# Attention, mixture of experts and soft experts on one core: w2 loaded first, p and phi issued by ScalarE, another order of the last output tiles

## Chip, cores and metric

The kernel runs on one core of one Trainium2 chip. The metric is the time of one execution on the device, in microseconds (us). The engines are TensorE (PE in the profile; its weight loads PEld), VectorE (DVE), ScalarE (ACT), GpSimd (POOL) and SyncE (SP, which only issues DMAs here). ScalarE and GpSimd issue some DMAs as well.

## The reference, cut to what matters

```
q, k, v: (4, 8, 576, 64)   p: (4, 8, 32, 64)   N = 4*576 = 2304, D = 512, F = 1024
sm_attn(a, b, c) = softmax(0.125 * a b^T) c
pk  = sm_attn(p, k, v)                       # 32 packed rows per head
x   = sm_attn(q, pk, pk), heads side by side # (2304, 512)
P   = domain_probs / (sum + 1e-9)            # (2304, 4)
x   = sum over 4 experts e of P[:, e] * (relu(x @ w1[e]) @ w2[e])
lg  = x @ phi                                # (2304, 32): 8 experts of 4 slots
d   = softmax of lg over the 2304 rows, c = softmax of lg over the 32 slots
slots = d^T @ x, expert by expert: relu(slots @ m1[e]) @ m2[e]   # m1 (8, 512, 1024), m2 (8, 1024, 512)
out = c @ slots                              # (2304, 512)
```

All of it is float32.

## The kernel before, in words

The kernel never forms the output x of the first mixture. Its product with phi is taken through `wphi` = w2[e] @ phi, 32 columns per expert, so that the hidden rows `ht` of the first mixture go straight to the logits. The work falls into a head, a main stage and a tail.

**Head** (lines 906 to 1014). The four batches go through one after the other; the head does attention for batch 0, in two groups of four heads (`attention`, g = 0 and 1), up to the point where the main loop can begin. The group's steps are: `kf` turns k on VectorE, `sa` the scores of p with k, `mx`, `ex`, `norm` the softmax, `et` its transposes, `pv` the product with v, `pk` its packing, `qf` and `sb` the scores of q, then a second softmax whose result is the operand `a2`. Beside them stands the work on `wphi` (`wphi_ops`, line 257): for each of eight half experts (1 MB of w2 each) 16 transposes on TensorE in four groups of four (`turn`, line 268), a copy by ScalarE per group (`put`, line 275), 32 small matmuls with phi (`project`, line 283), a copy, one transpose (line 299) and a copy. Four buffers hold w2; the load of a later half expert is issued by SP when the projection of the one four places earlier has been made. What of the wphi work is not placed in the head (`rest`) is dealt out in the first slots of the main loop, two ScalarE steps a slot.

The order of the head is made by `place_ops` (line 214): every step has an engine, a cost in us, the steps it depends on, the PSUM banks it takes and gives, and a rank (0 attention, 1 the first step of the main loop, 2 wphi). It places at each turn the step that can begin first, on ties the lower rank; a step that depends on another engine's begins 0.2 us after it. The result is one fixed order for each engine's queue; on the chip each engine runs its queue in that order and waits by semaphores. Loads are steps of SP with 2.5 us per MB, in the order of lines 928 to 941, behind a step `start`. After the head's steps SP issues p and k of batch 1 and part of its v (lines 1011 to 1014).

**Main stage** (line 1063). 128 slots. In slot s, `mm1(s)` makes 128 hidden features of one batch and expert with 12 matmuls (line 633); every fourth slot `make_g` (line 589) multiplies the packed values with the next 1 MB half of w1, for the next four slots. There is one w1 buffer: the next half is issued (line 183, by ScalarE) as the last step of `make_g`, and in program order `make_g(1)` stands right behind `mm1(0)`. `logits`, the softmaxes and the pooling of the previous batch are spread over the slots.

**Tail** (line 1113 on). From the start of batch 3, SP streams 80 chunks of 512 KB (w2, m1, m2) into whatever buffers come free (`load_chunk`). The last product (`slot_outputs`, line 1270) has two parts of 256 output columns; the chunks of the first part come first, four chunks of the second part last. For each part the kernel copies the accumulated rows (`so_sb`), sums them over four blocks with `rep` (`sr`), scales (`rr`) and then makes six output tiles, each of six matmuls (line 1316), three copies (`drain`) and one write of 384 KB by SP. `busy(n)` are n transposes whose result nobody reads.

Every DMA that SP or ScalarE issues takes one of eight semaphores in turn, and its issue waits until the transfer that had that semaphore before has landed.

Of the kernel before, what the change touches and what calls it, by code (L numbers as in the profile page):

```python
# [18 lines left out]
def tile_packed_attention_moe_softmoe(  # L19
# [28 lines left out]
    FC = 512  # L48
# [109 lines left out]
            )  # L158
        raw["v", b, g] = t

    def load_p(b):
        t = att_pool.tile([128, 4, D], F32, tag="p", name=f"p{b}")
        for a in range(2):
            for r in range(2):
                sp.dma_start(
                    t[64 * a + 32 * r : 64 * a + 32 * r + 32],
                    p[b].rearrange("(gh a) m d -> a m gh d", a=2)[a],
                )
        raw["p", b] = t
# [41 lines left out]
            self.deps, self.take, self.give, self.rank = list(deps), take, give, rank  # L211
            self.end = None

    def place_ops(ops, lag=0.2):


        free, banks_at, left = {}, [0.0] * 6, list(ops)
        while any(o.rank < 2 for o in left):
            ready = []
            for n, o in enumerate(left):  # L220
                spare = 2 if o.rank == 2 and o.take else 0
                if any(d.end is None for d in o.deps) or o.take + spare > len(banks_at):
                    continue
                t = max([d.end + lag * (d.eng != o.eng) for d in o.deps], default=0.0)
                if o.take:
                    t = max(t, sorted(banks_at)[o.take - 1])
                ready.append((max(t, free.get(o.eng, 0.0)), o.rank, n, o))
            first = min(ready, key=lambda c: c[:3])
            for t, rank, n, o in sorted(ready, key=lambda c: c[1:3]):
                if o.eng == first[3].eng and rank < first[1] and t < first[0] + 0.5 * first[3].cost:  # L230
                    first = (t, rank, n, o)
                    break
            t, _, n, o = first
            o.end = free[o.eng] = t + o.cost
            banks_at = sorted(banks_at)[o.take :] + [o.end] * o.give
            o.fn()
            left.pop(n)
        return left
# [8 lines left out]

    w2_t = {}

    def load_w2(n, t):  # L250
        e, hf = divmod(n, 2)
        sp.dma_start(
            t, w2[e, FC * hf : FC * hf + FC, :].rearrange("(x p) d -> p x d", p=128)
        )
        w2_t[n] = t

    def wphi_ops(n, loaded, next_load, done):
# [49 lines left out]
        def add(eng, cost, fn, deps, key, **kw):  # L307
            ops.append(Op(0, eng, cost, fn, deps, rank=2, key=n + key, **kw))
            return ops[-1]

        puts = []
        for x in range(4):
            tr = add("PE", 0.47, lambda x=x: turn(x), [loaded], 0.1 * x, take=1)
            puts.append(add("ACT", 0.58, lambda x=x: put(x), [tr], 0.1 * x, give=1))
        pr = add("PE", 1.3, project, puts, 0.5, take=1)
        if next_load:
# [589 lines left out]
    with tc.manual_schedule():  # L906
# [18 lines left out]
                i = 2 * g + hp  # L925
                load_qk(src, nm, b, g, hp, at and at[:, S * i : S * i + S])

        load("start", 0.9, lambda: None)
        load(("p", 0), 0.2, lambda: load_p(0))
        load(("k", 0), 0.6, lambda: load_two(k, "k", 0, 0))  # L930
        load(("k", 1), 0.6, lambda: load_two(k, "k", 0, 1))
        for g in range(2):
            load(("v", g), 0.8, lambda g=g: load_v(0, g, flat[1][:, 1536 * g : 1536 * g + 1536]))
        load(("q", 0), 0.6, lambda: load_two(q, "q", 0, 0, flat[0]))
        load("w2", 1.0, lambda: load_w2(0, w2s[0]))
        load(("q", 1), 0.6, lambda: load_two(q, "q", 0, 1, flat[0]))
        load("phi", 0.1, lambda: sp.dma_start(phi_sb, phi.rearrange("(c p) s -> p c s", p=128)))
        load("w1", 1.0, load_w1)
        load("w2_1", 1.0, lambda: load_w2(1, w2s[1]))
        for n in range(2, W2_BUFS):  # L940
            load(f"w2_{n}", 1.0, lambda n=n: load_w2(n, w2s[n]))

        make_identity(nc, ident)
        act.activation(out=den, in_=ident[:, 0:1], func=AF.Exp)
# [7 lines left out]
            rep[:, 0:96].rearrange("p (a s) -> p a s", a=3),  # L952
            st_i.unsqueeze(1).to_broadcast([128, 3, 32]),
        )
        busy(24)
        def head_tmp(tag, name):
            g = int(name[-1])
            if tag == "kt":
# [4 lines left out]
            n = (6 if name[0] == "n" else 4) + g  # L963
            return flat[2][:, S * n : S * n + S]

        ops.append(Op(0, "DVE", 0.45, lambda: flip_p(0), [loads["p", 0]]))
        att0 = [
            attention(0, g, head_tmp, lambda stage: None, (dve, pool)[g], loads) for g in range(2)
        ]
# [22 lines left out]
        def done():  # L992
            wphi_done[0] += 1

        landed = [loads["w2"]] + [loads[f"w2_{n}"] for n in range(1, W2_BUFS)]
        for n in range(NCH):
            after = None
            if n + W2_BUFS < NCH:
                m = n + W2_BUFS
                after = Op(  # L1000
                    0, "SP", 2.5, lambda m=m: load_w2(m, w2s[m % W2_BUFS]), [], rank=2
                )
                landed.append(after)
            ops += wphi_ops(n, landed[n], after, done)
        rest = sorted(place_ops(ops), key=lambda o: o.key)
        for o in list(rest):
# [263 lines left out]
        def slot_outputs():  # L1270
# [21 lines left out]
                busy(3)  # L1292
            return ended

        for p, (d0, dw) in enumerate(parts):
            ended = p > 0
            while not ended:
                ended = slot_outputs()
            so_sb = leftover(1, dw, d0)
            act.copy(so_sb, so[:, d0 : d0 + dw])  # L1300
            sr = mm_ps(f"sr{d0}")
            pe.matmul(sr[:, :dw], rep, so_sb, start=True, stop=True)
            rr = end[:, CHUNK : CHUNK + dw]
            act.mul(rr, sr[:, :dw], -1.0)
            for b2 in range(NB // 2):
                rows = out[2 * b2 * S : 2 * (b2 + 1) * S, d0 : d0 + dw].rearrange(
                    "(r x) d -> r x d", x=XR
                )
                cv = ct[:, b2].rearrange("p x b r t -> p x (b r t)")
                for j0 in range(0, XR, nt):  # L1310
                    jn = min(XR - j0, nt)
                    ob = out_tile()
                    ps = [mm_ps(f"o{d0}_{b2}_{j0}_{j}", keep=True) for j in range(jn)]
                    for j in range(jn):
                        o = slice(32 * j, 32 * j + 32)
                        pe.matmul(  # L1316
                            ps[j][:, :dw], cv[o, j0 + j], rr[o], start=True, stop=True,
                            tile_position=(32 * j, 0),
                        )
                    for j in range(jn):  # L1320
                        drain(ob[:, dw * j : dw * j + dw], ps[j][:, :dw])
                    let_go(ps)
                    sp.dma_start(
                        rows[:, j0 : j0 + jn, :],
                        ob[:, : dw * jn].rearrange("p (j d) -> p j d", d=dw),
                    )
                    if p == 0:
                        busy(2)
            while p == 0 and ck < len(chunks):
                slot_outputs()  # L1330


# [28 lines left out]
```

## Time and profile before

| | us |
|---|---|
| median of 3 runs (lowest to highest) | 505.82 (504.54 to 507.71) |
| the profiled execution | 501.07 |
| its span, first to last instruction | 499.3 |

| engine | busy us | share of the span |
|---|---|---|
| TensorE | 475.2 | 95% |
| VectorE | 295.3 | 59% |
| GpSimd | 197.3 | 40% |
| ScalarE | 182.5 | 37% |

The shares are averages over the whole span. A matmul's end is modelled, so a busy TensorE need not be at its peak. The granted clock is given as a share of 2.4 GHz; 0.50 is 1.2 GHz.

### The profile page before, as it was taken

To read this page: it belongs to the slowest core of one execution; us is meant where nothing else is said; L and a number is where in the kernel's file an instruction comes from. 1 tells how busy PE (TensorE), PEld (TensorE's weight loads), DVE (VectorE), ACT (ScalarE), POOL (GpSimd) and SP (SyncE) were. 2 spreads that over 40 slices of the span, in tenths; PEclk is the share of its full clock that TensorE was granted. 3 is DMA by queue.
4 is the path that set the end of the run, shared out by engine and by line. 5 is a ranking of instruction groups with operands and counts; after the bars stand their busy time and mean duration, and the time that the engine had idled before them with its cause. 6 is when DMAs were issued, how large, how long until landed. Compare 5 with 4: busy or idle time off the path is not lost.

```text
span 499.3 us, 13307 instructions
## 1 busy us (share of the span) xinstructions
PE 475.2 (95%) x5625; PEld 330.7 (66%) x5625; DVE 295.3 (59%) x557; ACT 182.5 (37%) x451; POOL 197.3 (40%) x250
## 2 busy tenths in 40 slices
PE   7798999999999999999999999999999999898884
PEld 4667887777775767788567787776787965231142
DVE  4683456687881778797558798872767632320022
ACT  1466655444440444445224444431434210110033
POOL 3022433356842445675325467641567502100000
PEclk9789999999999999999999999999999999899998
DMA  8979932655231356652214622393762689999996
GB/s 196 380 256 350 299 133 87 199 148 158 85 126 46 134 177 146 181 170 85 87 63 160 177 85 86 106 346 142 269 237 89 251 325 413 413 418 415 397 304 222
DMA packets 54667, 104.35 MB, mean 209 GB/s; under 512 B 5904, under 2 KB 20752, under 8 KB 54608
## 3 DMA queue, kind: packets, MB, share of 16 engines
q1 hardware_dynamic: 41280, 77.15, 44.2%
q10 hardware_dynamic: 13200, 26.22, 15.5%
q8 instruction: 44, 0.72, 0.6%
q0 software_dynamic: 128, 0.15, 0.2%
q14 instruction: 15, 0.12, 0.1%
HBM read 98.78 MB, written 4.72 MB: 207 GB/s over the span
## 4 chain that ended last, share of the span: by engine, by line
PE 69%; DMA 16%; DVE 8%; ACT 2%; SPq 1%; POOL 1%; issue 1%; ACTq 0%
PE h L633 35%; PE pb L794 8%; DMA hr<-in_moe_w_dram 8%; PE g L598 6%; PE lg L666 6%; DMA ck<-in_moe_w_dram 6%; PE pv L468 2%; PE sb L371 2%; PE w2t L268 2%; PE o L1316 2%; DMA p<-in_p_dram 2%; DVE hr L654 2%; DVE g L610 1%; PE sa L371 1%; DMA hr<-in_v_dram 1%; PE pw L283 1%
## 5 line engine op out<-in xcount | busy, mean ns | idle before, releaser
L633 PE MATMUL h<-a,g 128*128 128x288 f32 x1536 | 224.5, 300 | 0.6 <-DVE a L555 0.6
L633 PEld LDWEIGHTS h<-a,g 128*128 128x128 f32 x1536 | 206.7, 188 | 26.8 <-issue 14.7
L644 POOL TENSOR_TENSOR ht<-ht,work 128x288 f32<-128x288 f32 x191 | 154.5, 818 | 175.2 <-ACT ht L643 174.9
L643 ACT ACTIVATE ht<-h 128x288 f32<-128x288 f32 x191 | 78.5, 412 | 164.7 <-PE h L633 148.8
L654 DVE STREAM_TRANSPOSE hr<-ht 128x576 f32<-128x576 f32 x128 | 97.6, 764 | 37.4 <-POOL ht L644 34.8
L610 DVE TENSOR_TENSOR g<-g,g 128x512 fp32r<-128x512 f32 x64 | 41.2, 684 | 34.5 <-ACT g L608 34.5
L608 ACT CAST g<-g 128x512 fp32r<-128x512 f32 x64 | 34.5, 589 | 24.4 <-PE g L598 24.4
L638 DVE SCALAR_TENSOR_TENSOR ht<-h,work 128x288 f32<-128x288 f32 x65 | 28.6, 440 | 24.5 <-PE h L633 24.2
L666 PE MATMUL lg<-ht,wphi 128*32 128x288 f32 x512 | 38.7, 412 | 0.0
L666 PEld LDWEIGHTS lg<-ht,wphi 128*32 128x32 f32 x512 | 14.0, 109 | 33.1 <-POOL ht L644 23.3
L598 PE MATMUL g<-w,pkn 64*32 64x512 f32 x512 | 35.0, 603 | 0.2 <-DMA w<-in_moe_w_dram 0.2
L794 PE MATMUL pb<-hr,work 32*32 32x512 f32 x864 | 30.6, 598 | 0.0
L1265 DVE COPY ob<-o 128x256 f32<-128x256 f32 x9 | 3.5, 420 | 33.9 <-PE o L1316 33.9
L275 ACT COPY hr<-w2t 128x512 f32<-128x512 f32 x32 | 17.9, 597 | 7.4 <-PE w2t L268 7.4
L268 PE MATMUL w2t<-ident,hr 128*128 128x128 f32 x128 | 19.2, 292 | 1.1 <-DMA hr<-in_moe_w_dram 0.9
L794 PEld LDWEIGHTS pb<-hr,work 32*32 32x32 f32 x864 | 12.6, 103 | 11.4 <-issue 8.7
L268 PEld LDWEIGHTS w2t<-ident,hr 128*128 128x128 f32 x128 | 15.2, 148 | 4.9 <-issue 1.2
L686 POOL COPY work<-dpn 128x576 f32<-128x576 f32 x16 | 10.9, 680 | 13.6 <-DVE dpn L202 13.6
L808 DVE SCALAR_TENSOR_TENSOR tacc<-tacc,rsc,pb 128x512 f32<-128x512 f32 x12 | 8.2, 744 | 13.6 <-PE pb L794 13.6
L1280 PE MATMUL so<-hr 128*32 128x512 f32 (+1 forms) x68 | 13.7, 553 | 2.5 <-DMA hr<-in_moe_w_dram 2.3
L122 PE MATMUL busy<-ident 128*128 128x128 f32 x85 | 13.7, 307 | 1.4 <-POOL ident masks.py:199 1.4
L122 PEld LDWEIGHTS busy<-ident 128*128 128x128 f32 x85 | 10.7, 157 | 6.1 <-issue 4.2
(176 smaller groups left out, 442.7 us busy)
## 6 DMA issues: line engine op xcount, KB each, us to landing
w<-in_moe_w_dram ACTq DMA_DIRECT2D x25, 1024.0 KB, 5.1
ck<-in_moe_w_dram SPq DMA_DIRECT2D x42, 512.0 KB, 8.6
hr<-in_moe_w_dram SPq DMA_DIRECT2D x32, 512.0 KB, 9.9
hr<-in_moe_w_dram SPq DMA_DIRECT2D x8, 1024.0 KB, 10.9
w<-in_moe_w_dram SPq DMA_DIRECT2D x7, 1024.0 KB, 5.1
k<-in_k_dram SPq DMA_DIRECT2D x16, 288.0 KB, 4.4
v<-in_v_dram SPq DMA_DIRECT2D x18, 192.0 KB, 5.4
q<-in_q_dram SPq DMA_DIRECT2D x12, 288.0 KB, 3.0
```

What stands on the lines that cost most here:

```text
L122: pe.transpose(wp[:, :128], ident, ident)
L268: pe.transpose(st[x][:, 128 * dc : 128 * dc + 128], t[:, x, 128 * dc : 128 * dc + 128], ident,)
L598: pe.matmul(ps[g][c : c + 32, :], pkn_t[b][o : o + 64, g, hp, 0, :], t[o : o + 64, 2 * g + hp, :], start=True, stop=True, tile_position=(o ...
L608: act.copy(gg[:, 0, g], ps[g])
L610: dve.tensor_tensor(out=gg[:, 1, g], in0=ps[g], in1=gg[:, 0, g].bitcast(F32), op=ALU.subtract)
L633: pe.matmul(ps[:, :HS], gg[:, l, g, fs], m[:, ts], start=(g == 0 and i == 0), stop=(g == 1 and i == 2),)
L638: dve.scalar_tensor_tensor(out=ht[:, ts], in0=ps[:, :HS], scalar=0.0, in1=pr[:, ts], op0=ALU.max, op1=ALU.mult,)
L643: act.activation(out=ht[:, ts], in_=ps[:, :HS], func=AF.Relu)
L644: pool.tensor_tensor(out=ht[:, ts], in0=ht[:, ts], in1=pr[:, ts], op=ALU.mult)
L654: dve.transpose(out=hr[:, place(b, i), :, f0 : f0 + 32], in_=ht_t[s].rearrange("p (x t) -> p x t", t=32),)
L666: pe.matmul(lg_t[b][r][32 * x : 32 * x + 32, :HS], wphi[:, NFT * e + 4 * hf + x, :], ht_t[4 * ci + x][:, HS * r : HS * r + HS], start=(ch ...
L794: pe.matmul(pb[c][m : m + 32, :], d[o, x + par, :], hr[o, lo : hi + 1 : hi - lo, x + par, :], start=(x == 0), stop=(x == NBLK - 2), tile_p ...
```

## The change

Head: p and phi are issued by ScalarE at the beginning (`load_p(0, act)` and one more issue) instead of by SP; SP begins with the first MB of w2 in two halves, then k of both groups, the second MB of w2, and then v and q group by group, the third MB of w2, w1, the fourth MB. The costs of the loads in the plan are changed, and a step that depends on a load is placed 1.8 us after it instead of 0.2. The first two groups of transposes of w2's first MB depend on its first half alone. The filler at the start has 14 transposes instead of 24.

Tail: the six fillers of two transposes between the first part's tiles go. The second part's products, and the copy of their sum, come ahead of the first part's last two tiles instead of behind them.

```diff
-    def load_p(b):
+    def load_p(b, eng=sp):
...
-    def place_ops(ops, lag=0.2):
+    def place_ops(ops, lag=0.2, land=1.8):
...
-                t = max([d.end + lag * (d.eng != o.eng) for d in o.deps], default=0.0)
+                t = max(
+                    [d.end + (land if d.eng == "SP" else lag * (d.eng != o.eng)) for d in o.deps],
+                    default=0.0,
+                )
...
-            tr = add("PE", 0.47, lambda x=x: turn(x), [loaded], 0.1 * x, take=1)
+            tr = add("PE", 0.47, lambda x=x: turn(x), [loaded[x // 2]], 0.1 * x, take=1)
...
-        load("start", 0.9, lambda: None)
-        load(("p", 0), 0.2, lambda: load_p(0))
-        load(("k", 0), 0.6, lambda: load_two(k, "k", 0, 0))
+        load("start", 1.0, lambda: None)
+        load("p", 0.0, lambda: None)
+        load("w2_0a", 0.55, lambda: load_w2(0, w2s[0], (0, 2)))
+        load("w2_0b", 0.55, lambda: load_w2(0, w2s[0], (2, 4)))
+        load(("k", 0), 0.8, lambda: load_two(k, "k", 0, 0))
         load(("k", 1), 0.6, lambda: load_two(k, "k", 0, 1))
-        for g in range(2):
-            load(("v", g), 0.8, lambda g=g: load_v(0, g, flat[1][:, 1536 * g : 1536 * g + 1536]))
+        load("w2_1", 1.05, lambda: load_w2(1, w2s[1]))
+        load(("v", 0), 1.0, lambda: load_v(0, 0, flat[1][:, :1536]))
         load(("q", 0), 0.6, lambda: load_two(q, "q", 0, 0, flat[0]))
-        load("w2", 1.0, lambda: load_w2(0, w2s[0]))
+        load(("v", 1), 1.0, lambda: load_v(0, 1, flat[1][:, 1536:3072]))
         load(("q", 1), 0.6, lambda: load_two(q, "q", 0, 1, flat[0]))
-        load("phi", 0.1, lambda: sp.dma_start(phi_sb, phi.rearrange("(c p) s -> p c s", p=128)))
-        load("w1", 1.0, load_w1)
-        load("w2_1", 1.0, lambda: load_w2(1, w2s[1]))
-        for n in range(2, W2_BUFS):
-            load(f"w2_{n}", 1.0, lambda n=n: load_w2(n, w2s[n]))
+        load("w2_2", 1.05, lambda: load_w2(2, w2s[2]))
+        load("w1", 1.05, load_w1)
+        load("w2_3", 1.05, lambda: load_w2(3, w2s[3]))
+        load_p(0, act)
+        act.dma_start(phi_sb, phi.rearrange("(c p) s -> p c s", p=128))
...
-        busy(24)
+        busy(14)
...
+        def take_slots(d0, dw):
+            so_sb.append(leftover(1, dw, d0))
+            act.copy(so_sb[-1], so[:, d0 : d0 + dw])
+
+        while not slot_outputs():
+            pass
+        take_slots(*parts[0])
         for p, (d0, dw) in enumerate(parts):
-            ended = p > 0
-            while not ended:
-                ended = slot_outputs()
-            so_sb = leftover(1, dw, d0)
-            act.copy(so_sb, so[:, d0 : d0 + dw])
             sr = mm_ps(f"sr{d0}")
-            pe.matmul(sr[:, :dw], rep, so_sb, start=True, stop=True)
+            pe.matmul(sr[:, :dw], rep, so_sb[p], start=True, stop=True)
...
-                    if p == 0:
-                        busy(2)
-            while p == 0 and ck < len(chunks):
-                slot_outputs()
+                if p == 0 and n == len(tiles) - 3:
+                    while ck < len(chunks):
+                        slot_outputs()
+                    take_slots(*parts[1])
```

## Rows read from the trace of the kernel before

**Rows 1.** Stretches of 20 us: length, each engine's busy time, granted clock, DMA share, GB/s
```profile
60.00:80.00 20.00, 20.00 (x242) 16.77 (x241) 9.69 (x17) 10.82 (x26) 7.80 (x10) 1.00 0.29 105
...
380.00:400.00 20.00, 20.00 (x180) 17.06 (x181) 12.90 (x23) 6.85 (x16) 12.73 (x16) 1.00 0.51 190
```

**Rows 2.** Chain of waits, 36 to 45 and 385 to 424: start, us, what
```profile
36.71 7.78 DMA p<-in_p_dram
...
44.57 0.40 ACTq L183
...
413.27 10.45 DMA hr<-in_moe_w_dram
```

**Rows 3.** Timeline, TensorE and ScalarE's issues, 19 to 47: start, us, what, [idle before]
```profile
19.40 2.82 PE L268 MATMUL w2t<-ident,hr 128*128 128x128 f32 x12 [0.92 <-DMA hr<-in_moe_w_dram]
...
28.23 1.23 PE L598 MATMUL g<-w,pkn 64*32 64x512 f32 x16
...
29.39 1.53 PE L268 MATMUL w2t<-ident,hr 128*128 128x128 f32 x12
...
30.85 1.08 PE L283 MATMUL pw<-hr,tacc 128*32 128x128 f32 x32
...
33.93 0.43 ACTq L183 DMA_DIRECT2D w<-in_moe_w_dram  x1
...
39.26 1.86 PE L633 MATMUL h<-a,g 128*128 128x288 f32 x12
...
41.35 1.09 PE L598 MATMUL g<-w,pkn 64*32 64x512 f32 x16 [0.23 <-DMA w<-in_moe_w_dram]
...
46.13 1.06 PE L283 MATMUL pw<-hr,tacc 128*32 128x128 f32 x26 [1.05 <-ACT hr L275]
```

**Rows 4.** Shorter stretches, columns as in rows 1
```profile
2.00:6.00 4.00, 3.82 (x23) 3.58 (x21) 0.45 (x1) 0.23 (x2) 3.39 (x9) 1.00 0.77 166
26.00:28.00 2.00, 2.00 (x56) 0.74 (x36) 1.00 (x3) 0.00 (x0) 0.00 (x0) 0.50 1.05 402
428.00:430.00 2.00, 1.08 (x8) 0.97 (x8) 0.75 (x1) 0.00 (x0) 0.00 (x0) 1.00 1.03 416
431.40:434.70 3.30, 3.30 (x20) 0.85 (x16) 1.18 (x4) 1.74 (x4) 1.16 (x1) 0.50 1.02 406
```

**Rows 5.** DMA issues at 17.7, at 33.9, whole span: count, KB, us to landing
```profile
hr<-in_moe_w_dram SPq DMA_DIRECT2D x1, 1024.0 KB, 13.8
...
w<-in_moe_w_dram ACTq DMA_DIRECT2D x1, 1024.0 KB, 7.3
...
w<-in_moe_w_dram ACTq DMA_DIRECT2D x25, 1024.0 KB, 5.1
```

**Rows 6.** Costliest groups, whole span: count | busy us, mean ns | idle before
```profile
L275 ACT COPY hr<-w2t 128x512 f32<-128x512 f32 x32 | 17.9, 597 | 7.4 <-PE w2t L268 7.4
```

**Rows 7.** Timeline of TensorE, 478 to 494, columns as in rows 3
```profile
478.29 0.71 PE L1316 MATMUL o<-work,hr 32*128 32x256 f32 x6 [0.47 <-ACT work L1304]
...
485.02 1.93 PE L1280 MATMUL so<-ck,hr 128*32 128x256 f32 x32
487.45 0.70 PE L1302 MATMUL sr<-hr,rep 128*128 128x256 f32 x2 [0.49 <-ACT hr L1300]
488.62 4.55 PE L1316 MATMUL o<-work,hr 32*128 32x256 f32 x36 [0.47 <-ACT work L1304]
```

**Rows 8.** DMA issues at 473.2, 485.4, 490.0 and 493.7, columns as in rows 5
```profile
ck<-in_moe_w_dram SPq DMA_DIRECT2D x2, 512.0 KB, 8.6
...
out_dram<-hr SPq DMA_DIRECT2D x1, 384.0 KB, 4.1
...
out_dram<-hr SPq DMA_DIRECT2D x1, 384.0 KB, 2.4
...
out_dram<-work SPq DMA_DIRECT2D x1, 384.0 KB, 4.1
```

More of the change, by code (lines that the diff above doesn't have):

```diff
@@ L164, in load_p @@
             for r in range(2):
-                sp.dma_start(
+                eng.dma_start(
                     t[64 * a + 32 * r : 64 * a + 32 * r + 32],
@@ L248, in tile_packed_attention_moe_softmoe, with load_w2 @@
     w2_t = {}
-    def load_w2(n, t):
+    def load_w2(n, t, xs=(0, 4)):
         e, hf = divmod(n, 2)
+        xs = slice(*xs)
         sp.dma_start(
-            t, w2[e, FC * hf : FC * hf + FC, :].rearrange("(x p) d -> p x d", p=128)
+            t[:, xs],
+            w2[e, FC * hf : FC * hf + FC, :].rearrange("(x p) d -> p x d", p=128)[:, xs],
         )
@@ L964, in head_tmp @@
             return flat[2][:, S * n : S * n + S]
-        ops.append(Op(0, "DVE", 0.45, lambda: flip_p(0), [loads["p", 0]]))
+        ops.append(Op(0, "DVE", 0.45, lambda: flip_p(0), [loads["p"]]))
         att0 = [
@@ L993, in done @@
             wphi_done[0] += 1
-        landed = [loads["w2"]] + [loads[f"w2_{n}"] for n in range(1, W2_BUFS)]
+        landed = [(loads["w2_0a"], loads["w2_0b"])]
+        landed += [(loads[f"w2_{n}"],) * 2 for n in range(1, W2_BUFS)]
         for n in range(NCH):
@@ L1002, in tile_packed_attention_moe_softmoe @@
                 )
-                landed.append(after)
+                landed.append((after, after))
             ops += wphi_ops(n, landed[n], after, done)
@@ L1293, in slot_outputs @@
             return ended
-        for p, (d0, dw) in enumerate(parts):
-            ended = p > 0
-            while not ended:
-                ended = slot_outputs()
-            so_sb = leftover(1, dw, d0)
-            act.copy(so_sb, so[:, d0 : d0 + dw])
+        so_sb = []
+        def take_slots(d0, dw):
[4 more added lines that the diff above has]
+        take_slots(*parts[0])
+        for p, (d0, dw) in enumerate(parts):
             sr = mm_ps(f"sr{d0}")
-            pe.matmul(sr[:, :dw], rep, so_sb, start=True, stop=True)
+            pe.matmul(sr[:, :dw], rep, so_sb[p], start=True, stop=True)
             rr = end[:, CHUNK : CHUNK + dw]
             act.mul(rr, sr[:, :dw], -1.0)
-            for b2 in range(NB // 2):
+            tiles = [(b2, j0) for b2 in range(NB // 2) for j0 in range(0, XR, nt)]
+            for n, (b2, j0) in enumerate(tiles):
                 rows = out[2 * b2 * S : 2 * (b2 + 1) * S, d0 : d0 + dw].rearrange(
@@ L1309, in tile_packed_attention_moe_softmoe @@
                 cv = ct[:, b2].rearrange("p x b r t -> p x (b r t)")
[L1310 to L1325, printed above, removed]
-                    )
-                    if p == 0:
-                        busy(2)
-            while p == 0 and ck < len(chunks):
-                slot_outputs()
+                jn = min(XR - j0, nt)
+                ob = out_tile()
+                ps = [mm_ps(f"o{d0}_{b2}_{j0}_{j}", keep=True) for j in range(jn)]
+                for j in range(jn):
+                    o = slice(32 * j, 32 * j + 32)
+                    pe.matmul(
+                        ps[j][:, :dw], cv[o, j0 + j], rr[o], start=True, stop=True,
+                        tile_position=(32 * j, 0),
+                    )
+                for j in range(jn):
+                    drain(ob[:, dw * j : dw * j + dw], ps[j][:, :dw])
+                let_go(ps)
+                sp.dma_start(
+                    rows[:, j0 : j0 + jn, :],
+                    ob[:, : dw * jn].rearrange("p (j d) -> p j d", d=dw),
+                )
+                if p == 0 and n == len(tiles) - 3:
+                    while ck < len(chunks):
+                        slot_outputs()
+                    take_slots(*parts[1])
 _INS = ['q', 'k', 'v', 'p', 'moe_domain_probs', 'moe_w1', 'moe_w2', 'moe2_phi', 'moe2_w1', 'moe2_w2']
```

## Prediction

> **What bounds the kernel now.** I read the table of stretches first. From 60 us on TensorE is busy for 20.00 of 20 us [rows 1], and so it stays to about 400 us, so any real work that TensorE no longer has to do there, and any earlier start of that stage, comes off the end. Next the chain of waits. After 413.27 us it runs through DMAs alone [rows 2]: the stream of 512 KB chunks that feeds the last three products. That stream is started by buffers which the end of the main stage frees, so it moves as a whole with the main stage. Thus two stretches are left in which time can be won by ordering: the head, up to where the main loop runs without gaps (about 47 us), and the tail, from the landing of the first part's last chunk (476 us) to the last write.
>
> In the head the timeline shows TensorE waiting for data and then doing it in an unlucky order: at 19.40 it had waited 0.92 us for the first MB of w2, spends 2.82 us on twelve transposes of it, and only then begins group 1's product with v, which was ready [rows 3]. The DMA engines are the other half: 402 GB/s at a share of 1.05 when full, but a share of only 0.77 from 2 to 6 us [rows 4], about 4 x (1 - 0.77/1.05) = 1.07 us of transfer time unused. In the tail, the second part's 32 products stand behind all six output tiles of the first part and then pay a copy, a sum over slots and a scaling with nothing beside them [rows 7], while the writes stop between the two parts [rows 8].
>
> **Head, the order.** I followed place_ops with the new costs. On TensorE it gives: all 16 transposes of w2's first half MB pair and their projection, first part of attention (with one wait for phi ahead of it), 16 transposes of w2's second MB among the attention steps, the second projection, g of step 0, then 16 + 12 more transposes and two more projections, and mm1(0). Before, 15 groups of four transposes and three projections stood ahead of mm1(0); now 19 and four.
>
> **Head, work moved ahead.** Four more groups are 16 transposes at 1.53/12 = 0.13 us [rows 3]: 2.0 us. One more projection is 1.08 us [rows 3]. Together 3.1 us, which the main loop, where TensorE is never idle, no longer has. This counts in full if the time at which the main loop reaches a given point does not move.
>
> **Head, start of the loop.** The block of 0.92 + 2.82 us disappears from between the two products with v, a gain of at most 3.7 us for mm1(0), before at 39.26 [rows 3]. Against it, 1 MB of w2 now stands ahead of k and another ahead of v and q: at 402 GB/s each is 2.6 us; phi's 64 KB come on top, 1.07 us are won back. mm1(0) thus lies between 35.5 and about 39.5; I take 37.5. It is not what decides.
>
> What decides is make_g(1), right behind mm1(0) on TensorE, which needs the second half MB pair of w1. That load can be issued only after g of step 0 has used the one w1 buffer. The first w1 load is now followed by one MB only (w2's fourth). Before, the last load of the head landed at 17.7 + 13.8 = 31.5 us [rows 5]; with 1.07 us less idling it lands at 30.5, so w1 at 27.9, and g of step 0 stays at about 28.2, where it was [rows 3]. The next w1 issue was 5.7 us behind g, at 33.93 [rows 3]; ScalarE now has one w2 copy more ahead of it, 0.6 us [rows 6]: 34.5. It took 7.3 us to land, beside w2 loads on SP's queue [rows 5], and again has w2 loads beside it (the fifth, sixth and seventh, which no longer wait for a projection). So g(1) starts at 41.8, before at 41.35 [rows 3]: **a loss of 0.45 us**. Bounds of this landing: 5.1 us, the median over all ScalarE w1 loads [rows 5], which would put it at 39.6; and one further MB ahead of it, 2.6 us, which puts it at 44.4.
>
> **Head, one wait goes.** At 46.13 a projection had waited 1.05 us for a copy by ScalarE [rows 3], because ScalarE stood still until it could issue the third w1 load at 44.57, released by a p load that took from 36.71 to 44.5 [rows 2]. Those p loads now follow the seventh w2 load on SP, which is released by the third projection some 34 us in, and land before ScalarE comes to that issue. **1.05 us gained**; bound below 0 if p is as late again.
>
> **Head, the clock.** mm1(0) takes 1.86 us [rows 3] and ends at 39.4, so TensorE idles 2.4 us until g(1). In the window from 428 TensorE was busy for 1.08 of 2 us, and from 431.4 to 434.7 the granted clock was 0.50, which is 1.2 GHz [rows 4]. I expect the same fall here. Twelve transposes took 2.82 us at 0.50 and 1.53 at 1.00 [rows 3], so a stretch of 3.3 us at the lower level does the work of 1.8 us: **a loss of 1.5 us**; bounds 0 and 3 (two such stretches). The Trainium skill (TensorE: Matmul & The Clock Gate, HAM oscillation) ties the fall to waits for DMA longer than this one; by it the clock would hold and the sum be 1.5 us better. The 0.92 us without a matmul in the window from 428 were shorter and the clock still fell, so I keep the term.
>
> Head: 3.1 - 0.45 + 1.05 - 1.5 = 2.2 us.
>
> **Head, edits at nothing.** p and phi by ScalarE: five issues of 0.43 us [rows 3] and the table load behind them, ahead of ScalarE's first copy, which waits for w2 until about 5 us; that wait hides them, and without it they would cost about 2 us of ScalarE. SP loses those five issues. The warm-up of 14 instead of 24 transposes ends where w2's first half lands; if that lands late, the first transposes run at the lower level while TensorE waits for k anyway.
>
> **Tail.** Before, the first tile of part one begins at 478.29 and that of part two at 488.62: 10.33 us [rows 7]. After: four tiles at the pace of part two, which has no filler, 4.55/6 = 0.76 us: 3.0 us. Then 32 products, 1.93 us; their last chunk lands at 473.2 + 8.6 = 481.8 [rows 8], just as they get to it. Two more tiles, 1.5 us, which now cover the copy of the second part. Then the slot sum 0.70 and the scaling, 0.47 until the next tile as in [rows 7]: 1.2 us. Sum 7.6, so part two starts 2.7 us earlier on TensorE. The writes give some of that back. The last six land from 490.0 + 2.4 to 493.7 + 4.1 [rows 8], one per 1.07 us, slower than TensorE makes them; and the sixth write of part one landed at 485.4 + 4.1 = 489.5. If the first six end there again, the seventh lands at 490.6 instead of 492.4: 1.9 us. If they go out as fast as they are made, 2.7. I take 2.2 us, nearer to the row. With the six fillers gone the products and tiles themselves keep TensorE running.
>
> **Sum.** 2.2 + 2.2 = 4.4 us. The profiled execution took 501.07 us (span 499.3 and 1.8 around it), 0.9% under the median of the runs shown, 505.82; I take the 4.4 us off the median: **501.4 us**.
>
> **Rivals.** (a) The clock holds while TensorE waits for g(1): 5.9 us gained, 499.9. For it: ahead of 46.13 TensorE idled 1.05 us and the next 26 matmuls took 1.06 us, near the 1.08 us of 32 at 30.85 and not twice that [rows 3]; against it the fall after 428 [rows 4]. (b) w1's second load lands like the others, 5.1 us: g(1) follows mm1(0) at 39.6, a gain of 1.75 in place of a loss of 0.45 and no fall: 8.1 us, 497.7. Against it: SP's queue is full at that time. (c) The head gives nothing: a half-speed stretch falls on group 1's attention from about 22 us, as it did from 18 to 28 (0.50 at 26 us, [rows 4]), g(0) and everything behind it slip by 2 us; or writes give back the whole tail. About 2.2 us left: 503.6. (d) Slower: the early w2 loads delay w1. If the queues are served in the order of issue instead of taking turns, the second w1 load sits behind two MB of w2, 2 x 2.6 us, and lands at 47. g(1) loses 5.65 instead of 0.45, TensorE sits through two half-speed stretches, 3 us: head 3.1 + 1.05 - 5.65 - 3.0 = -4.5, with the tail 2.3 us slower: 508.1. It is slower than before from a landing at about 45 us. Against it: the p load on SP and the w1 load on ScalarE were in flight together, and w1, issued at 33.93 behind a w2 MB, landed in 7.3 us.
>
> **Chances.** The forecast 0.50, (a) 0.24, (b) 0.10, (c) 0.10, (d) 0.06. A measurement of this kernel can tell about 1% from no change, 5.06 us. (a) and (b) pass that, the forecast only at its upper edge: faster by over 1% 0.36, within 1% 0.58, slower by over 1% 0.06 at most, the end of (d). The range takes in (b) and (c) and the bounds of g(1): 497.7 to 505.0.
>
> **What would show it.** The transposes of w2's first MB lie before the first scores of attention; mm1(0) near 37.5; a gap in front of g(1) that a w1 load ends, near 41.8; the granted clock at 0.50 within 4 us behind it, or not; no gap before the fourth or fifth projection; part two's first tile 7.6 us behind part one's; the last write 1.9 to 2.7 us closer to the landing of the first part's last chunk. The prediction is wrong if TensorE does not wait for w1 at g(1), if phi's load holds up the first projection and with it the scores, or if the main stage shows new gaps.

## The result and the profile after

The changed kernel takes 504.29 us (median of 20 runs, 501.48 to 506.95), the kernel before 501.75 us beside it (20 runs, 497.62 to 507.71). The ratio is 1.0058, with the 95% interval [1.003, 1.0085]: slower by 0.6%, where 0.9% faster was forecast. Ratios leave out executions that took over 1.5% more than the fastest of their kernel. The profiled execution took 505.59 us with a span of 503.8, against 501.07 and 499.3.

The chain of waits of the changed kernel, 15 to 60 us, has two DMAs that the same stretch of before had not (start, us, what):

```profile
13.31 9.50 DMA hr<-in_v_dram
22.95 2.78 PE pv L473 x48
...
30.78 0.84 DVE hr L518 x2
...
34.80 0.79 DVE hr L549
...
36.25 2.04 ACT hr L280 x4
38.29 0.35 ACT g L613
38.68 9.88 DMA w<-in_moe_w_dram
48.69 1.96 PE g L603 x16
```

Between the two the chain runs through the second softmax of group 1 on VectorE, which begins late because the product with v was late, and through the copies and the cast that ScalarE has to make before it comes to the issue. The timeline of TensorE and ScalarE's issues shows the two DMAs as idle time of TensorE (start, us, what, [idle before]); the rows answer to [rows 3]:

```profile
4.52 2.62 PE L273 MATMUL w2t<-ident,hr 128*128 128x128 f32 x16
8.95 1.08 PE L288 MATMUL pw<-hr,tacc 128*32 128x128 f32 x32 [1.82 <-DMA tacc<-in_moe_phi_dram]
...
22.95 2.78 PE L473 MATMUL pv<-hr 96*64 96x32 f32 x48 [4.18 <-DMA hr<-in_v_dram]
...
27.76 1.78 PE L288 MATMUL pw<-hr,tacc 128*32 128x128 f32 x32
...
31.30 1.09 PE L603 MATMUL g<-w,pkn 64*32 64x512 f32 x16
...
36.88 0.66 PE L273 MATMUL w2t<-ident,hr 128*128 128x128 f32 x4 [1.73 <-ACT hr L280]
...
38.68 0.45 ACTq L183 DMA_DIRECT2D w<-in_moe_w_dram  x1
...
41.09 1.86 PE L638 MATMUL h<-a,g 128*128 128x288 f32 x12
48.69 1.96 PE L603 MATMUL g<-w,pkn 64*32 64x512 f32 x16 [5.74 <-DMA w<-in_moe_w_dram]
...
51.56 2.55 PE L638 MATMUL h<-a,g 128*128 128x288 f32 x12
```

What to see: the transposes of w2's first MB do lie early, but 4.18 us of waiting for v have taken the place of the block of 0.92 + 2.82 us that stood before group 1's product with v [rows 3]. g of step 0 is at 31.30 instead of 28.23, the second w1 load is issued at 38.68 instead of 33.93, and g(1) begins at 48.69 instead of 41.35 after a wait of 5.74 us. Short stretches show the clock and the DMA engines there (length, busy of PE, PEld, DVE, ACT, POOL, granted clock, DMA share, GB/s), as [rows 4]:

```profile
22.42:29.25 6.83, 6.30 (x108) 4.72 (x112) 3.87 (x10) 0.62 (x3) 0.67 (x1) 0.50 1.05 400
36.00:38.00 2.00, 1.12 (x24) 0.95 (x28) 1.93 (x6) 2.00 (x5) 1.13 (x1) 1.00 0.01 3
38.00:40.00 2.00, 2.00 (x34) 1.66 (x25) 1.85 (x3) 1.76 (x5) 0.35 (x1) 1.00 0.24 22
...
42.00:44.00 2.00, 0.95 (x8) 0.71 (x6) 0.00 (x0) 1.63 (x5) 0.59 (x1) 1.00 1.01 377
...
46.32:53.14 6.82, 4.45 (x27) 2.81 (x28) 1.80 (x3) 1.82 (x4) 0.00 (x0) 0.50 0.97 242
60.00:80.00 20.00, 20.00 (x238) 16.30 (x237) 9.92 (x16) 11.37 (x26) 7.21 (x9) 1.00 0.27 98
...
483.22:490.05 6.83, 6.83 (x52) 3.91 (x53) 2.45 (x6) 2.14 (x6) 0.00 (x0) 0.50 0.86 281
```

The clock falls to 0.50, the level of 1.2 GHz, within each of the two gaps (at 22.42 and at 46.32), and once in the tail. From 60 us on TensorE is as full as before [rows 1]. The DMA issues at 13.3 and 38.7 us and over the whole span, as [rows 5] (KB, us to landing):

```profile
hr<-in_v_dram SPq DMA_DIRECT2D x1, 192.0 KB, 9.5
...
w<-in_moe_w_dram ACTq DMA_DIRECT2D x1, 1024.0 KB, 9.9
...
w<-in_moe_w_dram ACTq DMA_DIRECT2D x25, 1024.0 KB, 5.1
```

The tail on TensorE, as [rows 7]:

```profile
483.01 4.50 PE L1328 MATMUL o<-work,hr 32*128 32x256 f32 x24 [0.47 <-ACT work L1316]
487.45 3.19 PE L1288 MATMUL so<-ck,hr 128*32 128x256 f32 x32
490.57 1.85 PE L1328 MATMUL o<-work,hr 32*128 32x256 f32 x12
492.35 0.70 PE L1314 MATMUL sr<-hr,rep 128*128 128x256 f32 x2
493.58 4.54 PE L1328 MATMUL o<-work,hr 32*128 32x256 f32 x36 [0.53 <-ACT work L1316]
```

The order is the new one, but 24 matmuls take 4.50 us where 36 take 4.54, and the 32 products 3.19 us instead of 1.93: they ran at the lower level. From the first part's first tile to the second part's it is 10.57 us, before 10.33.

To add it up I use a mark in the main loop, the start of mm1's group 16 (of its 128 of 12 matmuls each): 91.88 us before, 96.94 after. From group 8 to group 16 it is 26.78 us before and 23.91 after, so the work moved ahead is worth 2.9 us. Group 8 itself begins at 65.10 and at 73.03, 7.9 us later. And from the landing of the first part's last chunk to the end of the span ("tail" below) it is 23.35 us before and 23.13 after.

### The profile page after: what moved, and what is told of

Read it like the earlier page. It is cut to its first block, busy times and chain, and to the rows that moved or that the text cites. A ratio compares the mean times of both kernels' runs of the same rounds, so it can differ in the third digit from the quotient of the medians.

```text
span 503.8 us, 13274 instructions
## 1 busy us (share of the span) xinstructions
PE 474.0 (94%) x5603; PEld 330.7 (66%) x5603; DVE 295.2 (59%) x557; ACT 182.8 (36%) x451; POOL 197.1 (39%) x250
## 4 chain that ended last, share of the span: by engine, by line
PE 69%; DMA 18%; DVE 8%; ACT 2%; POOL 1%; issue 1%; SPq 1%; ACTq 0%
PE h L638 35%; PE pb L799 8%; DMA hr<-in_moe_w_dram 7%; PE g L603 6%; DMA ck<-in_moe_w_dram 6%; PE lg L671 6%; PE pv L473 2%; PE sb L376 2%; PE o L1328 2%; DMA w<-in_moe_w_dram 2%; DMA hr<-in_v_dram 2%; DVE hr L659 2%; DVE g L615 1%; PE sa L376 1%; PE w2t L273 1%; PE pw L288 1%
## 5 line engine op out<-in xcount | busy, mean ns | idle before, releaser
L615 DVE TENSOR_TENSOR g<-g,g 128x512 fp32r<-128x512 f32 x64 | 41.1, 683 | 40.5 <-ACT g L613 40.5
L613 ACT CAST g<-g 128x512 fp32r<-128x512 f32 x64 | 34.5, 590 | 27.3 <-PE g L603 27.3
L671 PE MATMUL lg<-ht,wphi 128*32 128x288 f32 x512 | 38.7, 412 | 0.0
L1288 PE MATMUL so<-ck,hr 128*32 128x256 f32 (+1 forms) x80 | 12.7, 547 | 1.9 <-DMA ck<-in_moe_w_dram 1.9
L603 PEld LDWEIGHTS g<-w,pkn 64*32 64x32 f32 x512 | 5.9, 105 | 11.1 <-issue 10.6
```

The costliest lines, as they stand in the source:

```text
L603: pe.matmul(ps[g][c : c + 32, :], pkn_t[b][o : o + 64, g, hp, 0, :], t[o : o + 64, 2 * g + hp, :], start=True, stop=True, tile_position=(o ...
L613: act.copy(gg[:, 0, g], ps[g])
L615: dve.tensor_tensor(out=gg[:, 1, g], in0=ps[g], in1=gg[:, 0, g].bitcast(F32), op=ALU.subtract)
L671: pe.matmul(lg_t[b][r][32 * x : 32 * x + 32, :HS], wphi[:, NFT * e + 4 * hf + x, :], ht_t[4 * ci + x][:, HS * r : HS * r + HS], start=(ch ...
L1288: pe.matmul(so[32 * c : 32 * c + 32, d0 : d0 + dw], hm[:, x + xl, 32 * i : 32 * i + 32], t[:, dw * xl : dw * xl + dw], start=(nx * n + xl ...
```

## Experiments

Two theories. **Order of loads:** with w2's second MB ahead of v, group 1 comes late; ScalarE, which works through its queue in order, issues the second w1 load late, and g(1) waits. **Rivals:** that load is slow because w2's seventh MB shares the DMA engines with it; or the change's other end, the tail, is what loses. Ratios are against before, with the 95% interval; spans, gaps and marks are of the profiled execution.

**1. The head alone**, in the order of before's tail.

```
- take_slots(*parts[0]), 4 tiles, slot_outputs(), 2 tiles
+ the output loop of before, with its fillers
```

> The change's head with the tail of before (fillers and order). Theory H (the whole loss is the head: group 1's v lands late, the second w1 load is issued 4.8 us later and lands at 48.6, and the clock falls twice): a time 2 to 5 us above before, g of step 1 between 46 and 49 us, and from the landing of the first part's last chunk to the end of the span 23.4 us as before (499.3 - 475.9). Rival T (head and tail share the loss, the tail by its lower clock): a time within 1.5 us of before.

505.86 us, ratio 1.0093 [1.005, 1.0136]. The gap ahead of pv is 3.66 us, that ahead of g(1) 5.53, group 16 begins at 96.05, the tail takes 22.9. The time is 3.4 us above before, as theory H had it: the head alone is the loss.

**2. The tail alone**: before's head with the new output loop.

```
- head of the changed kernel (loads, place_ops, w2 in halves)
+ head of before
```

> The head of before with the change's tail. Theory H: the time of before within 1 us, because what the new order saves (2.7 us by my sum) is lost to the granted clock at 0.50 from about 5 us behind the first part's last chunk on; chunk to end of span 23.1 us as in the changed kernel. Rival: the clock fell in the changed kernel by the chance of one execution; then it holds here, chunk to end is 20.5 to 21.5, and the time 2 to 2.7 us below before.

500.05 us, ratio 0.9948 [0.9903, 0.9992]. The timeline of its tail:

```profile
477.51 3.10 PE L1320 MATMUL o<-work,hr 32*128 32x256 f32 x24 [0.47 <-ACT work L1308]
480.55 1.93 PE L1280 MATMUL so<-ck,hr 128*32 128x256 f32 x32
482.41 1.85 PE L1320 MATMUL o<-work,hr 32*128 32x256 f32 x12
484.19 0.70 PE L1306 MATMUL sr<-hr,rep 128*128 128x256 f32 x2
485.42 4.55 PE L1320 MATMUL o<-work,hr 32*128 32x256 f32 x36 [0.53 <-ACT work L1308]
```

The rival came: the clock holds until the last tiles are done, with 7.91 us between the two first tiles and a tail of 20.99 us, 2.4 less than before. With experiment 1 the parts add to +0.93 - 0.52 = +0.41%, against +0.58% together, inside the intervals.

**3. Two fillers behind each tile of the first part**, in the changed kernel.

```
+                if p == 0:
+                    busy(2)
```

> The changed kernel with two filler transposes kept behind each of the first part's tiles. If the missing fillers let the clock fall: no 0.50 between the first part's last chunk and the second part's tiles, chunk to end of span about 21.5 (2 us less than the changed kernel's 23.1, less some 0.3 for four fillers that now cost time), and the time 1.5 to 2 us below the changed kernel. If the fillers don't matter: chunk to end 23.5 or more and the time that of the changed kernel or 0.5 above.

504.72 us, ratio 1.005 [1.0012, 1.0089]: no different from the change. The clock holds through the tiles and products (32 products in 1.93 us again), the first tiles are 9.64 us apart, the tail takes 22.2. Both expectations missed: the tail was to take 21.5 us, or 23.5 and more. Against experiment 2 (20.99) the fillers cost 1.2 of the 2.4 us that the new order gives. That they are what held the clock is not shown: in experiment 2 it held without them.

**4. The second w1 load right behind the first cast of g(0)**, in the changed kernel. The 16 products of that step, which read the one w1 buffer, stand ahead of both casts; the load no longer stands behind the second cast and what ScalarE has in between.

```
             act.copy(gg[:, 0, g], ps[g])
+            if ci == 0 and g == 0:
+                load_w1()
...
-        load_w1()
+        if ci:
+            load_w1()
```

> The changed kernel, but in the head the second w1 load is issued by ScalarE right behind the first copy of g of step 0 (at about 33 us instead of 38.7). Theory H: it lands at 39 to 41, before mm1(0) has ended (42.9), so the gap of 5.7 us ahead of g of step 1 goes and the clock does not fall behind it: 6 to 8 us below the changed kernel, 3 to 4 below before. Rival (the DMA engines are the bound there: w2's seventh MB and w1 need the same 8 us whenever they are issued): a gap of 3 us or more stays, and the time is within 3 us of the changed kernel.

498.02 us, ratio 0.988 [0.9828, 0.9932] (6 runs). Its timeline, TensorE:

```profile
22.85 2.77 PE L473 MATMUL pv<-hr 96*64 96x32 f32 x48 [3.70 <-DMA hr<-in_v_dram]
30.74 1.09 PE L603 MATMUL g<-w,pkn 64*32 64x512 f32 x16
...
40.53 1.86 PE L641 MATMUL h<-a,g 128*128 128x288 f32 x12
42.32 1.09 PE L603 MATMUL g<-w,pkn 64*32 64x512 f32 x16
```

Issued at 31.98, the load lands at 39.24. The wait for v is nearly as long as in the change (3.70 us), but g(1) follows mm1(0) without a gap, no low clock follows there, and group 16 begins at 88.98 instead of 96.94. From g(0) to group 16 it is 58.24 us instead of 65.65: of the 8.0 us, 7.4 come behind g(0), with the wait and the low clock that followed it.

**5. The same, with w2's second MB behind group 1's q.**

```
-        load("w2_1", 1.05, lambda: load_w2(1, w2s[1]))
         load(("v", 0), ...); load(("q", 0), ...); load(("v", 1), ...); load(("q", 1), ...)
+        load("w2_1", 1.05, lambda: load_w2(1, w2s[1]))
```

> e4_w1_early with w2's second MB moved from ahead of v to behind q of group 1. If the MB ahead of v is what keeps group 1's product with v waiting (3.7 us, to 22.85, in e4_w1_early): that gap falls to 1 us or less, mm1(0) begins at 37 to 38.5 instead of 40.5, and the time is 2 to 3 us below e4_w1_early. Rival (that MB's transposes filled waits that are there anyway): gaps of the same sum come up between the steps of attention, mm1(0) stays within 1 us, and the time too.

496.18 us, ratio 0.9922 [0.9884, 0.9961]. The head shows no low clock at all:

```profile
5.10:414.00 408.90, 398.62 (x5115) 298.58 (x5114) 280.88 (x516) 168.24 (x414) 191.07 (x235) 1.00 0.54 179
```

The gap ahead of pv is gone; 2.84 us of waiting for VectorE's softmax stand ahead of et instead, since the transposes that filled it have no data yet. g(0) begins at 28.20, group 8 at 60.84. But group 8 to 16 takes 26.8 us again: the work moved ahead is back in the main loop, so group 16 at 87.63 is only 1.35 us ahead of experiment 4. The time is not to be told from that of experiment 4.

**6. Before, with the early w1 load alone.**

```
 (the edit of experiment 4, in the kernel before)
```

> The kernel before with the early second w1 load alone. If the gain of e4_w1_early over before (4.4 us) comes from the w2 work that the change moves ahead and from the tail, and the w1 load was only what hid it: within 1 us of before, since g of step 1 waited 0.23 us for w1 there. Rival (the early w1 load is itself the gain): 3 to 4 us below before.

498.04 us, ratio 0.9937 [0.9901, 0.9972]. The load is issued at 28.30, lands in 6.7 us; the waits ahead of 41.35 and 46.13 us go, and group 16 begins at 89.35 instead of 91.88. Of these 2.5 us 1.2 are there at g(0) already (27.05 instead of 28.23), ahead of the edit; from g(0) to group 16 it is 62.30 us instead of 63.65. So the late issue cost the kernel before some 1.4 us already, against 7.4 after the change. The time, 3.6 us below before, is the rival's: the early load is a gain without the change's head.

**7. Without w2's seventh MB in the head**, in the changed kernel (it is loaded later).

```
+                if m == 6:
+                    after.deps.append(Op(0, "SP", 0.0, lambda: None, []))
```

> The changed kernel, but the load of w2's seventh MB is not placed in the head and comes behind the loads for batch 1. The second w1 load is still issued at about 38.5. If sharing the DMA engines with that MB makes it slow (9.9 us to land): it lands in 5 to 6 us, g of step 1 begins at 44 to 45 instead of 48.7, and the time is 3.5 to 6 us below the changed kernel. If the late issue is all: it still takes 8 us or more and the time is within 1 us of the changed kernel.

502.02 us, ratio 1.0019 [0.9987, 1.0051]. The second w1 load, its timeline row, and the DMA engines meanwhile:

```profile
w<-in_moe_w_dram ACTq DMA_DIRECT2D x1, 1024.0 KB, 9.4
```

```profile
47.77 1.96 PE L603 MATMUL g<-w,pkn 64*32 64x512 f32 x16 [5.25 <-DMA w<-in_moe_w_dram]
```

```profile
42.00:44.00 2.00, 0.53 (x4) 0.29 (x3) 0.00 (x0) 1.21 (x4) 1.02 (x2) 1.00 0.73 261
44.00:46.00 2.00, 0.00 (x0) 0.00 (x0) 0.00 (x0) 0.00 (x0) 0.52 (x1) 0.92 0.26 94
```

With the engines mostly idle from 44 us on, the load still takes 9.4 us. The first rival falls: without the w2 load beside it, it is hardly faster. In the tail, with the change's own code, the clock held until the last six tiles; it took 20.7 us, 2.4 less than the change's, about as much as the time is lower.

**8. Experiment 4 with one filler behind each tile of the first part.**

```
+                if p == 0:
+                    busy(1)
```

> e4_w1_early with one filler transpose behind each of the first part's tiles. If one is enough to hold the clock: no 0.50 in the tail, and from the landing of the first part's last chunk to the end of the span 21.3 to 21.8 us instead of 22.1. If the fall in the tail hangs on where its stretches lie in an execution and not on a filler: 22 us or more, or a fall all the same; the time within 1 us of e4_w1_early either way.

500.11 us, ratio 0.9968 [0.9928, 1.0008]: not better than experiment 4. In the profiled execution the clock falls all the same, though TensorE is full by the profile, and the tail takes 24.8 us:

```profile
475.00:478.00 3.00, 3.00 (x21) 1.76 (x21) 1.35 (x4) 1.21 (x4) 0.00 (x0) 1.00 0.81 263
478.01:484.84 6.83, 6.83 (x47) 2.90 (x47) 1.11 (x4) 1.32 (x5) 0.00 (x0) 0.50 0.61 200
```

**9. Experiment 7 with the second w1 load issued by SP** ahead of batch 1's v.

```
-        (act if 0 < n < (NB - 1) * NCH + 2 else sp).dma_start(
+        (act if 1 < n < (NB - 1) * NCH + 2 else sp).dma_start(
...
-        load_w1()                # end of make_g
+        if ci:
+            load_w1()
...
+        load_w1()
         load_v(1, 0)
```

> e7_no_seventh_w2 with the second w1 load issued by SP behind batch 1's k, at about 38.2 us as there, instead of by ScalarE. If ScalarE's queue is what makes that load slow (9.4 us to land with nearly nothing beside it): it lands in 5 to 6 us, g of step 1 begins at 43.5 to 44.5. If it is the time and place (the DMA engines come up late one by one behind a lull): 8 us or more again, g of step 1 at 46 or later, and the time within 1 us of e7_no_seventh_w2.

499.68 us, ratio 0.9972 [0.9929, 1.0014]. Issued at 37.33 it takes 7.1 us, between the 9.4 of experiment 7 and the 5.1 of the median w1 load; g(1) waits 2.68 us and group 16 begins at 92.35. The row of g(1), and the clock behind the wait:

```profile
44.52 1.85 PE L603 MATMUL g<-w,pkn 64*32 64x512 f32 x16 [2.68 <-DMA w<-in_moe_w_dram]
```

```profile
44.72:48.13 3.41, 3.41 (x24) 1.82 (x9) 1.12 (x2) 1.70 (x4) 0.00 (x0) 0.50 1.06 325
```

Whether the other queue or the 0.9 us earlier issue makes it faster, this run doesn't say.

**10. The change with w2's second MB behind group 1's q**, the w1 load where the change has it.

```
-        load("w2_1", 1.05, lambda: load_w2(1, w2s[1]))     # ahead of v of group 0
+        load("w2_1", 1.05, lambda: load_w2(1, w2s[1]))     # behind q of group 1
```

> The changed kernel with w2's second MB behind q of group 1, and the second w1 load where the change has it. If the wait for group 1's v is the root of the late w1 issue: that wait goes, w1 is issued at 33.5 to 35 instead of 38.7, and half or more of the gap of 5.7 us ahead of g of step 1 goes; 2 to 5 us below the changed kernel. Rival (the issue is late because more copies of w2 stand ahead of it on ScalarE): issued at 36 us or later, the gap stays at 4 us or more, and the time is within 2 us of the changed kernel.

498.68 us, ratio 0.995 [0.991, 0.9989]. Its timeline, TensorE and ScalarE's issue, and the DMA issue at 34.4:

```profile
17.25 1.89 PE L437 MATMUL et<-ident,hr 128*96 128x128 f32 x12 [2.99 <-DVE ss L426]
19.07 5.34 PE L473 MATMUL pv<-hr 96*64 96x32 f32 x96
...
29.78 1.09 PE L603 MATMUL g<-w,pkn 64*32 64x512 f32 x16
...
34.45 0.39 ACTq L183 DMA_DIRECT2D w<-in_moe_w_dram  x1
...
40.10 1.09 PE L603 MATMUL g<-w,pkn 64*32 64x512 f32 x16
```

```profile
w<-in_moe_w_dram ACTq DMA_DIRECT2D x1, 1024.0 KB, 5.1
```

One line of the change is moved. v's last load lands at 19.10 instead of 22.82, both groups' products with v run in one go, and since the planner reckons with the loads, the second projection now falls behind g(0). The w1 load goes out at 34.45 (forecast for the change: 34.5) and g(1) at 40.10 waits for nothing. That is 1.1% off the changed kernel (0.995/1.0058). The place of that load, with the order of work that follows from it, is the cause of the late issue. How much of it is the wait for v itself is not separated: ScalarE's order changed too. Between the two casts of g(0) it makes six copies of w2 in the change, two before and none here, so the rival's copies went along with the wait.

**11. Experiment 6 with the new tail.**

```
 (the edit of experiment 4 in the kernel before, and the output loop of the change)
```

> e6_before_w1_early with the change's tail. If head and tail add up: 2.4 us below e6_before_w1_early where the tail's clock holds, 0 to 1.2 where it falls; 1.0% below before. If the order of the change's head is worth its 3 us once w1 is early, this is 1 to 3 us above e5_v_before_w2 and e4_w1_early; if not, level with them.

496.29 us, ratio 0.9917 [0.9873, 0.9961]; span 492.9, the lowest of all profiled, with a tail of 21.4 us. It does without the new head altogether and is level with experiments 4 and 5: the new head's order shows no gain once w1 is early.

**12. Experiment 4 with w2's second MB between group 1's v and q.**

```
         load(("v", 1), ...)
+        load("w2_1", 1.05, lambda: load_w2(1, w2s[1]))
         load(("q", 1), ...)
```

> e4_w1_early with w2's second MB between v and q of group 1. If both terms can be had (no wait for v, and the w2 work still done ahead of the main loop): mm1(0) at 37 to 39 with the work left of e4_w1_early, 1 to 3 us below it and 1.5% below before. If q of group 1, now 2.6 us later, takes the place of v: a wait ahead of group 1's second scores, and the time of e4_w1_early within 1 us.

497.41 us, ratio 0.9954 [0.9914, 0.9993], group 16 at 90.80. The wait ahead of et is 2.90 us as in experiment 5, and the clock is low from 16.02 to 29.68. No better than experiments 4 and 5.

Experiments 4, 5, 11 and 12, all about 0.5 to 1.2% under before, can't be told apart by their intervals; any of them beats both kernels.

## Why the prediction was wrong

**The step that failed is "Head, start of the loop", and in it the sentence that "g of step 0 stays at about 28.2".** I took that time from the landing of the first w1 load (forecast 27.9, in fact 29.10) and so let one input stand for the whole step. TensorE comes to g(0) only behind group 1's product with v, its scores and, newly, a second projection. I had listed that projection in TensorE's order and seen that two MB of w2 now lie ahead of v, but charged both to mm1(0) alone, and even that began at 41.09, outside the 35.5 to 39.5 that I gave it. v's last load landed at 14.66 us before and lands at 22.82 now. Then the slip grows step by step:

- Group 1's product with v begins at 22.95, before at 22.15: 0.8 us, since the wait for v has only taken the place of the w2 block.
- From there to g(0) 8.35 us instead of 6.08: the second projection stands among the scores and takes 1.78 us, in part at the lower level. g(0) at 31.30, not 28.2.
- From g(0) to the w1 issue 7.4 us, not 6.3: I had one copy of w2 more ahead of the issue, but between the two casts of g(0) ScalarE makes six instead of two, stands 1.00 us for VectorE's softmax and makes a cast of its result; TensorE itself waits 1.73 us for a copy. Issue at 38.68, not 34.5.
- Landing after 9.9 us, not 7.3. I had 5.1 and one more MB (9.9) as bounds; the upper one came. Beside the load lay w2's seventh MB, which had slipped as well (issued at 38.66): from 41 to 46 us SP's queue moved 0.89 MB and ScalarE's 0.99. But by experiment 7 the load is hardly faster without that MB.
- g(1) at 48.69, not 41.8; bounded at 44.4, so outside. Against before it is 0.8 + 2.3 + 1.7 + 2.6 = 7.3 us: v, the way from there to g(0), from g(0) to the issue, the landing.

**Its sum.** For the head I had 3.1 - 0.45 + 1.05 - 1.5 = +2.2 us. Measured: from group 8 to 16 2.9 us less, for the work moved ahead; start of g(1) -7.3 in place of -0.45; the wait at 46.13 is gone, +1.05 (right: no gap ahead of a projection after 41 us); low clock behind g(1) about -1.6 (g 1.96 instead of 1.09, mm1 2.55 instead of 1.83). That gives -5.0, and group 16 begins 5.06 us later.

**Its largest gain.** The 3.1 us for work moved ahead had a condition, that the time at which the main loop reaches a given point does not move, and that failed as well. Without any wait for w1 mm1(0) still begins at 40.53 (experiment 4) and 40.24 (8), with the head of before at 38.47 (6) and 37.20 (11). Group 16 follows at 88.98 and 88.25, against 89.35 and 88.07: what the main loop saves, the head spends. Two profiles of the same head lie up to 1.3 us apart in this mark, so no gain of the new head can be read from it. Experiment 10 has the start of the loop as forecast (mm1(0) at 37.85 for 37.5, the issue at 34.45 for 34.5), and group 16 at 90.14; but from group 8 to 16 it takes 26.79 us, as before, so there the work is not moved ahead. No run had both.

**Clock.** The fall came (from 46.32, forecast within 4 us behind mm1(0)'s end at 42.95), against rival (a), but within a wait of 5.74 us and not of 2.4. For that wait the trace agrees with the Trainium skill (TensorE: Matmul & The Clock Gate, HAM oscillation), which ties such falls to longer DMA waits. Experiment 9 had nearly the wait that I reckoned with, 2.68 us, and the clock fell there too, to 0.50 from 44.72 to 48.13, as my term had it. By that section of the Trainium skill it would have held; the measurement decides. In the tail, where the longest wait was 0.49 us, the clock fell as well, as it did after 428 us in the kernel before [rows 4]. The Trainium skill (TensorE: Matmul & The Clock Gate, A second HAM failure mode: psum-queue depth-cycling) has a second case, a kernel that idles a little between groups of matmuls, and it is nearer to this. In experiment 8, though, TensorE was busy for 3.00 of 3.00 us by the profile ahead of the fall.

**Tail.** The order and its size were right wherever the clock held up to the second part's tiles: 7.91 us between first tiles in experiments 2, 5, 7, 11 and 12 (forecast 7.6), and 2.4 us gained in experiment 2 (forecast 2.2). Wrong was the sentence that "the products and tiles themselves keep TensorE running": in the profiled change, and in experiments 4, 9 and 10, the clock fell in between, and in the change it took 2.1 of 2.4 us back. I had removed six pairs of fillers at a price of nothing without naming a price if their cover was needed. Whether they give cover is open. With two fillers behind each tile none of four profiles shows the fall (before, 1, 3, 6), without them four of nine do, with one filler (8) the only one does. Falls included, the nine tails without fillers take 21.7 us in the mean, the tail of experiment 3 with them 22.2.

**phi.** It held the first projection back by 1.82 us (landed 8.82), so the edit put at nothing was not quite that. But the last k loads land at 10.71, and the second half of the first scores has to wait for those in any case; no run separated the two.

**Rivals.** (d) had the right place and nearly the right landing (47; in fact 48.56), and its threshold, slower from a landing at about 45, fits the change (slower) and experiment 9 (landing at 44.39, not slower); experiment 7 lands at 47.64, and its 1.0019 is within the noise. Its mechanism was wrong. It had the queues served in the order of issue; from 41 to 46 us both moved data side by side (0.99 and 0.89 MB). The load was issued 4.2 us later than forecast, and was slow even with no w2 beside it. I gave it 0.06 because I argued against the mechanism, and missed that the same place can fail through another cause. (c) described the half-speed stretch on group 1's attention, which came (22.42 to 29.25), but at 2 us of slip where 3.1 followed.

**The base.** I took 4.4 us off a median of three runs, 505.82. The median of 20 is 501.75. Taken off that, the same 4.4 us give 497.4, and the range ends at about 501: that 504.29 lies inside the stated range, 497.7 to 505.0, is owed to the high base and no merit of the forecast.

**Still open:** why a w1 load issued by ScalarE at 38 us takes 9.4 to 9.9 us and one issued at 34.45 takes 5.1. In the change SP's queue takes half of the DMA engines' time; in experiment 7 that does not explain it: from 40.5 us on hardly anything but this load moves there, 1.00 MB up to 47 us, 159 GB/s in the mean. In experiment 7 the first of the 16 DMA engines was done with it at 43.17 and the last at 47.64; in experiment 10 they were done within 0.3 us, at 39.23 to 39.52.

## What to carry to other kernels

When a load is moved ahead, follow the loads that it pushes back to the instruction that uses them, and from there along every in-order engine to the next DMA that this engine issues: here 2 MB ahead of v moved the product with v by 0.8 us, and the start of g(1), 26 us later behind a w1 load, by 7.3. Before trusting a step's new time, list everything that it stands behind, not only its own input. Work moved ahead of a point is a gain only as far as the engine would have stood idle there: here the main loop saved 2.9 us and, with the wait for w1 gone, still began 2 to 3 us later than with the old head. And an edit that takes fillers out puts the clock at risk; that belongs in the sum, with bounds, even if the work around looks dense.

## What the runs showed of the hardware

- **The granted clock goes with most of the scatter of one kernel.** Over the 85 runs of the kernel before that stand beside the experiments and count in their ratios, the mean clock of an execution goes from 0.967 to 0.997 and the time from 497.65 to 506.81, with a correlation of -0.81. Medians by clock, before against after: under 0.975, 504.73 (11 runs) and 505.43 (10); 0.975 to 0.985, 502.66 (31) and 502.84 (8); above, 499.95 (43) and 502.49 (2). The change has the lower clock more often, in 10 of 20 runs under 0.975 against 23 of all 98; the fall behind the wait for g(1) is part of that. This is a correlation, which no run has tested by itself.
- **The fall in the tail differs between executions of like code.** With the same output loop it lay at 483.22 to 490.05 in the change, at 478.78 to 482.19 in experiment 4, and ahead of the last matmul nowhere in experiments 2, 5 and 12.
- **After a lull the DMA engines moved little in the first microsecond behind an issue.** With loads issued at 38.66 and 38.68 they moved 22 GB/s from 38 to 40 us, 279 from 40 to 42 and 377 from 42 to 44 in the change; with one issued at 34.45, 14 GB/s from 34 to 36 and 334 from 36 to 38 in experiment 10.
- **The 16 engines drift apart.** v's last load in the change landed on the first engine at 19.75, on 15 of them by 20.42 and on the last at 22.82, and the product with v began at 22.95.
